# One pool of PSUM banks for attention and experts, gathers into row tiles, and a new order of the last picks

## The chip, the cores and the metric

The kernel runs on one core of one Trainium2 chip. The metric is the device time of one execution in microseconds (us), the median of several runs; smaller is better. The engines are named as in the profile: PE is TensorE, DVE is VectorE, ACT is ScalarE, POOL is GpSimd, SP is SyncE.

## The reference

The reference chains three steps over 1536 tokens of 512 features.

1. Retention-like linear attention: per head, `state = gamma * state + outer(k, v)`, `y = q @ state / 8`, over 2 batches, 8 heads, 768 positions, 64 features a head.
2. A first mixture of 8 experts with a skip: tokens with `x @ w_skip > 0` go to the expert with the largest gate logit, `relu(x @ w1) @ w2` (512 to 1024 to 512), are scaled by the gate's softmax and added to `x`; the others pass unchanged.
3. A second mixture of 8 experts on the result, without skip and without adding `x`: each expert takes its tokens in their order up to a capacity of 384, and the rest become zero.

```python
logits = xc @ w_gate
e_idx = np.argmax(logits, axis=1)
...
h = np.maximum(xc[mask] @ w1[e], 0.0)
y[mask] = gate_w[mask, None] * (h @ w2[e])
...
out[do_compute] = xc + y
```

## The kernel before, in words

**Attention.** The 768 positions are six chunks of 128, each with two batches: twelve units. `attention` (L459) holds a generator `main` (L580) and calls `step_side` after each of its yields; `step_side` moves the side generators on by one step. So the order of instructions on every engine is the order in which the program text emits them, and the number of yields decides where a side step falls. The last unit emits, in this order: the matmuls with the running state (L554), a yield, the first step of chunk 5's side generator (its first logits, L256), the matmuls with v (L564), a yield.

**Routing while attention runs.** For each chunk `route_tokens` (L369) makes the side generator `sink` (L370). Its steps are: token rows and gate logits of each batch into the row tile `rowc` (L256, L260); `pick` (L273): maximum, mask `m` of the picked expert, softmax gate into the row tile; `mrow` (L394), the table's row numbers; `write_rows` (L320) on ACT's DMA queue, which writes the chunk's 256 rows of 580 floats to `table` in device memory; the rank of each token in its expert (`ranked`, L299), the slot `sl` and the one-hot `hot` (L354); and four matmuls (L441) that turn `hot` and `mrow` into the table's row number for each slot, added into `idacc`. `idle(n)` stands for n empty steps. After chunk 4 the first block of the first expert is gathered into `a0` (L446) with the rows known by then; the rows of chunk 5 that belong to it are added by matmuls with a one-hot `oh` (`places`, L346; `place`, L337, L341), so that the first block doesn't wait for a gather.

**Pools.** Attention's SBUF pool `a_p` and PSUM pool `psa` close with `at.close()` (L626). Then the pools for gathered blocks (`xs_p`), more raw weights (`raw2`), split weights (`w2`) and activations (`m_p`) open in the same space, and a PSUM pool `ps` for the experts. What comes first in such a pool waits until everything in the pools closed before is done, the table writes out of `rowc` among it. In both phases eight banks are used: 5 for scores, 1 for the state, 2 for the rest in attention; 3 for transposes (`t`), 3 for layer 1 (`s`), 2 for layer 2 (`o`) in the experts.

**First experts.** POOL gathers the block of each expert e from `table` by an indirect DMA (`gather`, L326, L331) into a tile of `xs_p`, in the order 1, 0, 2, 3 (L797). Per expert: layer 1 (L672) with three matmuls for each product (high and low halves of a 32-bit value, `mm3`, L663), transposes of its result and of the next expert's block (`split_T`, L649, L658), layer 2 of the expert before (L686). Weights stream through SP's queue into `raw` (L175), ACT copies the high part (L225), DVE subtracts for the low part (L233).

**Second experts.** After layer 2 of expert e, `route_b` (L698) makes the expert's result rows in `row2[e % 2]`, picks the second expert, writes the 128 rows to `table` on POOL's queue (L324) and adds the new row numbers to `idb`. The first expert of the second mixture has two blocks; the second of them consists of rows of experts 0 to 7. Rows of experts 0 to 5 come from a late gather issued by expert 6's `route_b` (L741), those of experts 6 and 7 are placed by matmuls with `ohb` (`place_b0`, L837). `load_held` (L178) lets the weight loads go on that `load_w` holds back from the 39th on. From expert 1 on, two blocks go through together (`pair_T`, `pair_layer1`, `pair_layer2`), and results leave by an indirect DMA of POOL (L307).

Of the kernel before, what the change touches and what calls it, by code (L numbers as in the profile page):

```python
# [7 lines left out]
F32 = mybir.dt.float32  # L8
# [19 lines left out]
HOLD = 38  # L28
NW, NW2 = 4, 2
AWAY = 4096.0  # L30
C_GQ, C_MASK, C_GV = 0, 512, 640
# [13 lines left out]
def kernel(  # L45
# [22 lines left out]
    a_p = at.enter_context(tc.tile_pool(name="a", bufs=2))  # L68
    psa = at.enter_context(tc.tile_pool(name="psa", bufs=2, space=bass.MemoryType.PSUM))

# [201 lines left out]

    def pick(lg, nt, ng, rm, gate_out):  # L273

# [16 lines left out]
        nc.vector.tensor_tensor(out=m, in0=t[:, :, 0:8], in1=tm.to_broadcast([128, n, 8]), op=ALU.is_equal)  # L291
        se = sm.tile([128, nt, ng, 1], F32, tag=f"se{n}", name="se")
        nc.vector.tensor_reduce(out=se, in_=ex.rearrange("p (a g) j -> p a g j", a=nt), axis=AX.X, op=ALU.add)
        se2 = sm.tile([128, nt, ng], F32, tag=f"sf{n}", name="sf")
        nc.vector.tensor_scalar(out=se2, in0=se.rearrange("p a g o -> p a (g o)"), scalar1=1e-9, scalar2=None, op0=ALU.add)
        nc.vector.reciprocal(out=gate_out, in_=se2)
        return m
# [71 lines left out]
    def route_tokens(rows, rows_p):  # L369
        def sink(c, xt, psum):  # L370
# [3 lines left out]
            def pt():  # L374
                return psum("s", 5)

# [17 lines left out]
            nc.vector.tensor_tensor(  # L394
                out=mrow, in0=m4, in1=cs[:, C_ROW + B * c:C_ROW + B * c + B].unsqueeze(2).to_broadcast([128, B, 16]), op=ALU.mult
            )
# [61 lines left out]

    def attention(a_p, ps, first, nbuf, sink, pump, g_tiles):  # L459
        units = [(c, b) for c in range(NCH) for b in range(B)]  # L460
# [4 lines left out]

        def psum(tag="m", bufs=2):
            return ps.tile([128, 512], F32, tag=tag, bufs=bufs, name=tag)

        u = ps.tile([128, 512], F32, tag="u", bufs=1, name="u")
        if pump:  # L470
            warm(psum("s", 5), 11)
        nc.tensor.matmul(out=u, lhsT=zb[:, 0:128], rhs=zb[:, 0:512], start=True, stop=True, skip_group_check=True)
# [36 lines left out]
        def scores(c, b):  # L509
            qq = ain[c][:, 0, b].rearrange("p (r t) -> p r t", r=4)  # L510
            kk = ain[c][:, 1, b].rearrange("p (r t) -> p r t", r=4)
            sa = [psum("s", 5), psum("s", 5)]
            for r in range(4):
                for j in range(2):
                    nc.tensor.matmul(  # L515
                        out=sa[j][:, 128 * r:128 * r + 128], lhsT=kk[64 * j:64 * j + 64, r, :],
                        rhs=qq[64 * j:64 * j + 64, r, :], start=True, stop=True,
                    )
                if r == 1:
                    yield  # L520
            p = []
            for j in range(2):
                t = a_p.tile([128, 4, 128], F32, tag=f"p{j}", name="p")
                nc.vector.tensor_tensor(  # L524
                    out=t, in0=sa[j].rearrange("p (r t) -> p r t", r=4),
                    in1=mask.unsqueeze(1).to_broadcast([128, 4, 128]), op=ALU.mult,
                )
                p.append(t)
            pt[c, b] = p
            yield  # L530
# [94 lines left out]
    attention(a_p, psa, first, 3, route_tokens(rowc, a_p), True, [(a_p, "g2")] + 2 * [(x_p, "xh"), (x_p, "xl")])  # L625
    at.close()  # L626

    ps = fast.enter_context(tc.tile_pool(name="ps", bufs=2, space=bass.MemoryType.PSUM))
    xs_p = fast.enter_context(tc.tile_pool(name="xs", bufs=NXS))
# [3 lines left out]

    def psum(tag="t", bufs=3):
        return ps.tile([128, 512], F32, tag=tag, bufs=bufs, name=tag)

# [35 lines left out]
    def layer1(x, kind, e, mid=None):  # L672
        h = m_p.tile([128, FF], F32, tag="h", name="h", bufs=1)
        for j in range(2):
            acc = psum("s", 3)
            w = wt[kind, e, j]
# [9 lines left out]
    def layer2(hT, kind, e, mid=None):  # L686
        acc = psum("o", 2)
        for k in range(FT):
# [9 lines left out]
    def route_b(e, xs, acc, lead, rest):  # L698
# [48 lines left out]
        yield  # L747

# [132 lines left out]
    def pair_layer1(x, e):  # L881
        hs = []
        for j in range(2):
# [3 lines left out]
            for g in (0, 2):  # L887
                acc = psum("s", 3).rearrange("p (f t) -> p f t", f=2)
                for f in range(2):
# [13 lines left out]
    def pair_layer2(hs, e):  # L903
        acc = [psum("o", 2), psum("o", 2)]
        for c in range(2):
# [7 lines left out]

    x = late[3]
    emit_out(xs2[0, 0], acc)
# [21 lines left out]
    def general(gctx):  # L937
# [15 lines left out]
        with (  # L953
            tc.tile_pool(name="ga", bufs=2) as ga_p,
            tc.tile_pool(name="gps", bufs=2, space=bass.MemoryType.PSUM) as gps,
        ):
            attention(ga_p, gps, load_chunk(0, ga_p, 2), 2, sink, False, [(ga_p, f"g2{c}") for c in range(1, NCH)])
        ps = gctx.enter_context(tc.tile_pool(name="ps2", bufs=2, space=bass.MemoryType.PSUM))
# [14 lines left out]
        def dense(w1, w2):  # L973
            for e in range(E):
# [5 lines left out]
                for g in range(NTILE // 4):  # L980
# [10 lines left out]
                    for a in range(4):  # L991
                        t = 4 * g + a
                        yp = psum("o", 2)
                        for f in range(FT):
# [128 lines left out]
```

## Time and profile before

| | us |
|---|---|
| median of 3 runs | 396.45 (396.05 to 396.46) |
| the profiled execution's own time | 396.63 |
| its span, from the first to the last instruction | 394.9 |
| PE busy in the span | 377.5 (96%) |
| DVE busy | 260.6 (66%) |
| ACT busy | 216.4 (55%) |
| POOL busy | 69.8 (18%) |

A page of the profile gives busy times, the chain of work that ended last, and groups of instructions; the trace can be asked for an engine's instructions in order of time, for waits and who released them, and for DMA issues. A line of a timeline has the start, the duration, the engine, the line of the kernel, the operation, what it writes and reads, and how many instructions it stands for; in brackets stand the idle time before it and what ended it. PEld is the loading of weights into PE, which lies beside its matmuls. Ends of matmuls are modelled: neighbours overlap by about 0.1 us.

### The profile page before, as it was taken

What the parts mean: (1) busy time and instruction counts of PE and PEld (TensorE: products, weight loads), DVE (VectorE), ACT (ScalarE), POOL (GpSimd) and SP (SyncE); (2) the same over time, 40 slices, a digit from 0 to 9 for tenths busy, and PEclk for the clock granted to TensorE, in tenths of its full rate; (3) what the DMA queues carried; (4) which work ended last, traced back from release to release, by engine and by line L of the source; (5) the groups of instructions that cost most, each with busy time, mean ns of one, the idle gap of its engine ahead of it and who ended that gap; (6) DMA issues with size and microseconds to landing.
All of it is one profiled execution on the core that took longest, in us unless ns stands there. A gap on an engine that the chain in (4) does not pass through costs nothing.

```text
span 394.9 us, 6637 instructions
## 1 busy us (share of the span) xinstructions
PE 377.5 (96%) x2616; PEld 322.9 (82%) x2616; DVE 260.6 (66%) x481; ACT 216.4 (55%) x283; POOL 69.8 (18%) x97
## 2 busy tenths in 40 slices
PE   8899999879999999999999999999999999999992
PEld 3788878667877877877778898988989899898982
DVE  2668995558999999999863868374574737455110
ACT  1547773177878777877543845545545555542201
POOL 6310010180011010000046020403013040311101
PEclk9999999999999999999999999999999999999998
DMA  8999993299999998889975486849566683320101
GB/s 301 403 420 417 377 337 147 91 343 373 374 349 337 339 365 289 338 299 314 310 274 142 176 288 233 277 146 314 175 233 187 221 285 127 139 62 0 53 2 41
DMA packets 18137, 97.69 MB, mean 247 GB/s; under 512 B 2991, under 2 KB 3119, under 8 KB 8628
## 3 DMA queue, kind: packets, MB, share of 16 engines
q1 hardware_dynamic: 12180, 80.03, 56.4%
q0 software_dynamic: 4000, 13.25, 9.8%
q10 hardware_dynamic: 1920, 3.93, 2.7%
q8 instruction: 22, 0.36, 0.3%
q14 instruction: 15, 0.12, 0.1%
HBM read 88.11 MB, written 10.14 MB: 249 GB/s over the span
## 4 chain that ended last, share of the span: by engine, by line
PE 77%; DMA 7%; issue 6%; ACT 5%; DVE 3%; POOL 1%; ACTq 0%; POOLq 0%; DVEq 0%
PE o L665 11%; PE s L665 10%; PE o L667 10%; PE s L667 10%; PE s L666 10%; PE o L666 10%; DMA cs<-in_cst_dram 4%; PE t L658 3%; PE s L256 2%; ACT hi L205 2%; DMA xs<-table,ida 2%; PE t L241 2%; PE t L876 1%; PE m L564 1%; ACT ain L502 1%
## 5 line engine op out<-in xcount | busy, mean ns | idle before, releaser
L233 DVE TENSOR_TENSOR lo<-raw,hi 128x2048 fp32r<-128x2048 f32 x60 | 136.3, 2284 | 5.9 <-ACT hi L225 4.5
L225 ACT ACTIVATE hi<-raw 128x2048 fp32r<-128x2048 f32 x60 | 114.8, 1914 | 18.1 <-PE o L667 15.3
L665 PE MATMUL o<-hi,hTh 128*128 128x512 f32 x192 | 78.2, 407 | 0.2 <-ACT hTh L361 0.2
L667 PE MATMUL o<-hi,hTl 128*128 128x512 f32 x192 | 75.5, 393 | 0.0
L666 PE MATMUL o<-lo,hTh 128*128 128x512 f32 x192 | 74.9, 390 | 0.0
L666 PE MATMUL s<-xl,hi 128*128 128x256 f32 x224 | 63.2, 282 | 0.0
L667 PE MATMUL s<-xh,lo 128*128 128x256 f32 x224 | 63.1, 282 | 0.0
L665 PE MATMUL s<-xh,hi 128*128 128x256 f32 x224 | 63.1, 282 | 0.0
L896 DVE SCALAR_TENSOR_TENSOR hTl<-s,hTh 128x512 fp32r<-128x512 f32 x28 | 19.4, 692 | 63.9 <-ACT hTh L895 63.9
L307 POOL DMA_INDIRECT out_dram<-y,ixo x16 | 20.4, 1275 | 143.4 <-ACT y L751 131.0
L667 PEld LDWEIGHTS o<-hi,hTl 128*128 128x128 f32 x192 | 36.0, 188 | 8.8 <-DVE hTl L362 0.7
L666 PEld LDWEIGHTS s<-xl,hi 128*128 128x128 f32 x224 | 42.7, 191 | 0.3
L665 PEld LDWEIGHTS s<-xh,hi 128*128 128x128 f32 x224 | 42.7, 191 | 0.3
L667 PEld LDWEIGHTS s<-xh,lo 128*128 128x128 f32 x224 | 42.6, 190 | 0.0
L665 PEld LDWEIGHTS o<-hi,hTh 128*128 128x128 f32 x192 | 36.1, 188 | 6.7 <-ACT hTh L361 0.5
L666 PEld LDWEIGHTS o<-lo,hTh 128*128 128x128 f32 x192 | 36.2, 188 | 6.6
L895 ACT ACTIVATE hTh<-s 128x512 fp32r<-128x512 f32 x28 | 16.7, 598 | 40.8 <-PE s L667 40.5
L665 PE MATMUL s<-hi,xh 128*128 128x512 f32 x80 | 33.4, 417 | 1.2 <-DVE xl L362 0.9
L667 PE MATMUL s<-hi,xl 128*128 128x512 f32 x80 | 31.5, 394 | 0.0
L666 PE MATMUL s<-lo,xh 128*128 128x512 f32 x80 | 31.3, 392 | 0.0
L751 ACT ACTIVATE y<-o,xs 128x512 f32<-128x512 f32 x15 | 10.3, 690 | 32.9 <-PE o L667 25.2
L524 DVE TENSOR_TENSOR p<-s,cs 128x512 f32<-128x512 f32 x24 | 15.4, 683 | 12.7 <-PE s L515 12.7
(148 smaller groups left out, 509.9 us busy)
## 6 DMA issues: line engine op xcount, KB each, us to landing
raw<-in_w1a_dram SPq DMA_DIRECT2D x16, 1024.0 KB, 6.9
raw<-in_w2a_dram SPq DMA_DIRECT2D x16, 1024.0 KB, 6.5
raw<-in_w1b_dram SPq DMA_DIRECT2D x16, 1024.0 KB, 5.6
raw<-in_w2b_dram SPq DMA_DIRECT2D x16, 1024.0 KB, 5.0
ain<-in_qkv_dram SPq DMA_DIRECT2D x10, 1024.0 KB, 10.0
table<-rowc ACTq DMA_DIRECT2D x6, 580.0 KB, 3.8
table<-row POOLq DMA_DIRECT2D x8, 290.0 KB, 6.4
ain<-in_qkv_dram SPq DMA_DIRECT2D x4, 512.0 KB, 6.0
```

Source lines behind the costliest of these rows:

```text
L205: nc.scalar.activation(out=hi[:, k], in_=r3[:, k], func=ACTF.Copy)
L225: nc.scalar.activation(out=hi, in_=r3, func=ACTF.Copy)
L233: nc.vector.tensor_tensor(out=lo, in0=r3, in1=hi.bitcast(F32), op=ALU.subtract)
L307: return nc.gpsimd.indirect_dma_start(out=dst[:, :], out_offset=bass.IndirectOffsetOnAxis(ap=idx, axis=0), in_=src, in_offset=None, bounds ...
L524: nc.vector.tensor_tensor(out=t, in0=sa[j].rearrange("p (r t) -> p r t", r=4), in1=mask.unsqueeze(1).to_broadcast([128, 4, 128]), op=ALU.mult,
L658: nc.tensor.transpose(t[:, 128 * k:128 * k + 128], src[:, w * (4 * g + k):w * (4 * g + k) + 128], ident)
L665: nc.tensor.matmul(out=acc, lhsT=a[0], rhs=w[0], start=first, stop=False)
L666: nc.tensor.matmul(out=acc, lhsT=a[0], rhs=w[1], start=False, stop=False)
L667: nc.tensor.matmul(out=acc, lhsT=a[1], rhs=w[0], start=False, stop=last)
L751: nc.scalar.activation(out=y, in_=acc, func=ACTF.Copy, scale=xs[:, GCOL + 1:GCOL + 2])
L895: nc.scalar.activation(out=hi[:, g:g + 2, :], in_=acc, func=ACTF.Relu)
L896: nc.vector.scalar_tensor_tensor(out=lo[:, g:g + 2, :], in0=acc, scalar=0.0, in1=hi[:, g:g + 2, :].bitcast(F32), op0=ALU.max, op1=ALU.subtract
```

## The change

1. One PSUM pool `ps` with four tags of 3, 2, 1 and 2 banks serves both phases; `bank` takes the tags of a use in turn. Attention's `psum` becomes `attention_bank`.
2. In the last chunk `pick` leaves the gate (sum, add, reciprocal) to a later call; gate, `mrow` and the table write of chunk 5 come behind the two `places`.
3. In chunk 4 one empty step less stands ahead of the slot numbers (L441) and of `a0`'s gather.
4. The gathers of experts 1 and 0 go into `row2[1]` and `row2[0]`, which are there from the start. Their `route_b` then works in place and leaves out the copy of the token number.
5. Expert 6's rows are no longer placed by matmuls: the late gather comes behind the update of `idb` with expert 6's rows, its range holds them, and `place_b0` has one `place` and one step less. `load_held` moves with the gather.

```diff
+BANKS = {"a": 3, "b": 2, "c": 1, "d": 2}
...
-    psa = at.enter_context(tc.tile_pool(name="psa", bufs=2, space=bass.MemoryType.PSUM))
+    ps = fast.enter_context(tc.tile_pool(name="ps", bufs=2, space=bass.MemoryType.PSUM))
+    turns = {}
+
+    def bank(name, *tags):
+
+        i = turns[name] = turns.get(name, -1) + 1
+        tag = tags[i % len(tags)]
+        return ps.tile([128, 512], F32, tag=tag, bufs=BANKS[tag], name=name)
+
+    def attention_bank(name="m"):
+        return bank(name, *{"s": "aaabb", "u": "c", "m": "d"}[name])
...
-    def pick(lg, nt, ng, rm, gate_out):
+    def pick(lg, nt, ng, rm, gate_out, later=None):
...
-        se = sm.tile([128, nt, ng, 1], F32, tag=f"se{n}", name="se")
...
-        nc.vector.reciprocal(out=gate_out, in_=se2)
+
+        def gate():
+            se = sm.tile([128, nt, ng, 1], F32, tag=f"se{n}", name="se")
...
+            nc.vector.reciprocal(out=gate_out, in_=se2)
+
+        if later is None:
+            gate()
+        else:
+            later.append(gate)
         return m
...
-            m = pick(lg, 2, 2, None, rc[:, :, GCOL:GCOL + 2])
+            later = [] if last else None
+            m = pick(lg, 2, 2, None, rc[:, :, GCOL:GCOL + 2], later)
...
-            write_rows(nc.scalar, rc, B)
-            yield
+
+            def row_numbers():
...
+                write_rows(nc.scalar, rc, B)
+
             if not last:
+                row_numbers()
+                yield
                 yield from idle(1 if c == NCH - 2 else 2)
...
                     places(oh[:, b, :], sl[:, b:b + 1], m4[:, b, 0:1])
+                later[0]()
+                row_numbers()
...
             if not last:
-                yield from idle(2 if c == NCH - 2 else 3)
+                yield from idle(1 if c == NCH - 2 else 3)
...
-    def psum(tag="t", bufs=3):
-        return ps.tile([128, 512], F32, tag=tag, bufs=bufs, name=tag)
+    def psum(name="t"):
+        return bank("e" + name, *{"t": "a", "s": "cbb", "o": "d"}[name])
...
-        nc.vector.tensor_copy(out=r2[:, IDCOL:IDCOL + 1], in_=xs[:, IDCOL:IDCOL + 1])
+        if xs is not r2:
+            nc.vector.tensor_copy(out=r2[:, IDCOL:IDCOL + 1], in_=xs[:, IDCOL:IDCOL + 1])
...
-        if e >= E - 2:
+        if e == E - 1:
             oh = sm.tile([128, 128], F32, tag="ohb", name="ohb", bufs=2)
             places(oh, sl, m[:, 0:1])
             late.append((r2, oh))
-        if e == E - 2:
-            late.insert(0, gather(numbers(idb[:, 0:1], "id0"), 1 + NT + 128 * e))
-            load_held()
         yield
...
         nc.vector.tensor_tensor(out=idb, in0=idb, in1=new[:, 0:E], op=ALU.add)
+        if e == E - 2:
+            late.append(gather(numbers(idb[:, 0:1], "id0"), 1 + NT + 128 * E - 128))
+            load_held()
         yield
...
-    xs1 = {e: gather(ida[:, e:e + 1], 1 + NT) for e in (1, 0, 2, 3)}
+    xs1 = {e: gather(ida[:, e:e + 1], 1 + NT, row2[e] if e < 2 else None) for e in (1, 0, 2, 3)}
...
-        place(acc, *late[2], False, False)
-        yield
         place(acc, late[0], ident, False, True)
...
-    x = late[3]
+    x = late[2]
```

The rest of the diff renames the calls of `psum` to the new form and gives the fallback `general` banks of its own.

## Rows read from the trace of the kernel before

**Rows 1.** Busy times by stretch: us, busy of each engine (instructions), PE clock, DMA share, GB/s.

```profile
60.00:80.00 20.00, 17.48 (x150) 14.27 (x148) 10.95 (x49) 5.45 (x13) 3.01 (x7) 1.00 0.31 109
```

**Rows 2.** PE's waits over the span: us in total, times, longest us.

```profile
PE t L658 <- DMA xs<-table,ida: 1.6, 1, 1.6
...
PE s L665 <- DVE xl L362: 0.9, 1, 0.9
```

**Rows 3.** PE's timeline between 52 and 100 us.

```profile
65.82 1.14 PE L554 MATMUL m<-ain,sbd 128*128 128x128 f32 x8
...
69.19 0.61 PE L441 MATMUL s<-mrow,hot 128*128 128x16 f32 x4
...
70.88 1.89 PE L456 MATMUL s<-zb 128*128 128x512 bf16 x8
...
73.07 0.17 PE L304 MATMUL s<-m,ones 128*128 128x16 bf16 x1
...
85.08 0.60 PE L658 MATMUL t<-cs,h 128*128 128x128 f32 x4
87.32 0.66 PE L658 MATMUL t<-cs,xs 128*128 128x128 f32 x4 [1.65 <-DMA xs<-table,ida]
```

**Rows 4.** The chain that ended last, 50 to 100 us: start, us, what.

```profile
70.64 3.83 DMA a<-table,id
...
79.34 7.94 DMA xs<-table,ida
```

**Rows 5.** DVE's timeline between 60 and 100 us.

```profile
67.28 0.61 DVE L356 TENSOR_SCALAR hot<-iota,sl 128x256 fp32r<-128x256 f32 x2
...
73.28 0.18 DVE L296 RECIPROCAL rowc<-sf 128x4 f32<-128x4 f32 x1
...
73.53 0.18 DVE L409 TENSOR_TENSOR pr<-s,m 128x32 f32<-128x32 f32 x1
...
74.55 0.29 DVE L350 TENSOR_SCALAR oh<-iota,sl 128x128 f32<-128x128 f32 x1
```

**Rows 6.** ACT's timeline between 60 and 100 us; ACTq is its DMA queue.

```profile
73.57 0.37 ACTq L324 DMA_DIRECT2D table<-rowc  x1
...
78.88 3.72 ACT L225 ACTIVATE hi<-raw 128x2048 fp32r<-128x2048 f32 x2
```

**Rows 7.** DMA issues on the page: count, KB each, median us to landing.

```profile
table<-rowc ACTq DMA_DIRECT2D x6, 580.0 KB, 3.8
table<-row POOLq DMA_DIRECT2D x8, 290.0 KB, 6.4
...
xs<-table,ida POOLq DMA_INDIRECT x15, 4.5
```

**Rows 8.** POOL's timeline between 180 and 226 us.

```profile
195.14 0.54 POOL L324 DMA_DIRECT2D table<-row  x1 [14.09 <-DVE mrowb L725]
198.30 2.37 POOL L331 DMA_INDIRECT xs<-table,id  x1 [2.62 <-PE t L745]
...
207.74 1.02 POOL L331 DMA_INDIRECT xs<-table,idbi  x1 [4.37 <-DMA table<-row]
```

**Rows 9.** DVE's timeline between 180 and 226 us.

```profile
197.39 0.15 DVE L315 CAST id<-idb 128x1 int32<-128x1 f32 x1
```

**Rows 10.** Waits of SP's DMA queue from 60 to 100 us: total, times, longest.

```profile
SPq L175 <- DMA table<-rowc: 20.1, 1, 20.1
```

**Rows 11.** SP's timeline between 60 and 100 us.

```profile
78.70 0.33 SPq L175 DMA_DIRECT2D raw<-in_w1a_dram  x1
```

**Rows 12.** PE's timeline between 186 and 226 us.

```profile
204.93 1.05 PE L341 MATMUL t<-ohb,row 128*128 128x128 f32 x8
...
207.21 1.05 PE L341 MATMUL t<-ohb,row 128*128 128x128 f32 x8
...
217.82 1.04 PE L876 MATMUL t<-cs,xs 128*128 128x128 f32 x8
```

**Rows 13.** PE's timeline between 0 and 12 us.

```profile
1.53 4.76 PE L456 MATMUL s<-zb 128*128 128x512 bf16 x11 [1.53 <-DVE zb L91]
```

More of the change, by code (lines that the diff above doesn't have):

```diff
@@ L291, in pick @@
         nc.vector.tensor_tensor(out=m, in0=t[:, :, 0:8], in1=tm.to_broadcast([128, n, 8]), op=ALU.is_equal)
-        se = sm.tile([128, nt, ng, 1], F32, tag=f"se{n}", name="se")
-        nc.vector.tensor_reduce(out=se, in_=ex.rearrange("p (a g) j -> p a g j", a=nt), axis=AX.X, op=ALU.add)
-        se2 = sm.tile([128, nt, ng], F32, tag=f"sf{n}", name="sf")
-        nc.vector.tensor_scalar(out=se2, in0=se.rearrange("p a g o -> p a (g o)"), scalar1=1e-9, scalar2=None, op0=ALU.add)
-        nc.vector.reciprocal(out=gate_out, in_=se2)
+        def gate():
+            se = sm.tile([128, nt, ng, 1], F32, tag=f"se{n}", name="se")
+            nc.vector.tensor_reduce(out=se, in_=ex.rearrange("p (a g) j -> p a g j", a=nt), axis=AX.X, op=ALU.add)
+            se2 = sm.tile([128, nt, ng], F32, tag=f"sf{n}", name="sf")
+            nc.vector.tensor_scalar(out=se2, in0=se.rearrange("p a g o -> p a (g o)"), scalar1=1e-9, scalar2=None, op0=ALU.add)
+            nc.vector.reciprocal(out=gate_out, in_=se2)
[3 more added lines that the diff above has]
+            later.append(gate)
         return m
@@ L374, in pt @@
             def pt():
-                return psum("s", 5)
+                return psum("s")
             lg = sm.tile([128, B, 17], F32, tag="lg", name="lg")
@@ L393, in sink @@
             mrow = sm.tile([128, B, 16], F32R, tag="mrow", name="mrow")
-            nc.vector.tensor_tensor(
-                out=mrow, in0=m4, in1=cs[:, C_ROW + B * c:C_ROW + B * c + B].unsqueeze(2).to_broadcast([128, B, 16]), op=ALU.mult
-            )
-            write_rows(nc.scalar, rc, B)
-            yield
+            def row_numbers():
+                nc.vector.tensor_tensor(
+                    out=mrow, in0=m4, in1=cs[:, C_ROW + B * c:C_ROW + B * c + B].unsqueeze(2).to_broadcast([128, B, 16]), op=ALU.mult
+                )
+                write_rows(nc.scalar, rc, B)
             if not last:
+                row_numbers()
+                yield
                 yield from idle(1 if c == NCH - 2 else 2)
@@ L456, in warm, with attention @@
             nc.tensor.matmul(out=acc, lhsT=zb[:, 0:128], rhs=zb[:, 0:512], start=True, stop=True)
-    def attention(a_p, ps, first, nbuf, sink, pump, g_tiles):
+    def attention(a_p, psum, first, nbuf, sink, pump, g_tiles):
         units = [(c, b) for c in range(NCH) for b in range(B)]
@@ L511, in scores @@
             kk = ain[c][:, 1, b].rearrange("p (r t) -> p r t", r=4)
-            sa = [psum("s", 5), psum("s", 5)]
+            sa = [psum("s"), psum("s")]
             for r in range(4):
@@ L624 @@
             nc.gpsimd.memset(t[:, :, KW * k + 128:KW * k + KW], 0.0)
-    attention(a_p, psa, first, 3, route_tokens(rowc, a_p), True, [(a_p, "g2")] + 2 * [(x_p, "xh"), (x_p, "xl")])
+    attention(a_p, attention_bank, first, 3, route_tokens(rowc, a_p), True, [(a_p, "g2")] + 2 * [(x_p, "xh"), (x_p, "xl")])
     at.close()
-    ps = fast.enter_context(tc.tile_pool(name="ps", bufs=2, space=bass.MemoryType.PSUM))
     xs_p = fast.enter_context(tc.tile_pool(name="xs", bufs=NXS))
@@ L674, in layer1 @@
         for j in range(2):
-            acc = psum("s", 3)
+            acc = psum("s")
             w = wt[kind, e, j]
@@ L686, in layer2 @@
     def layer2(hT, kind, e, mid=None):
-        acc = psum("o", 2)
+        acc = psum("o")
         for k in range(FT):
@@ L887, in pair_layer1 @@
             for g in (0, 2):
-                acc = psum("s", 3).rearrange("p (f t) -> p f t", f=2)
+                acc = psum("s").rearrange("p (f t) -> p f t", f=2)
                 for f in range(2):
@@ L903, in pair_layer2 @@
     def pair_layer2(hs, e):
-        acc = [psum("o", 2), psum("o", 2)]
+        acc = [psum("o"), psum("o")]
         for c in range(2):
@@ L956, in general, with general_bank @@
         ):
-            attention(ga_p, gps, load_chunk(0, ga_p, 2), 2, sink, False, [(ga_p, f"g2{c}") for c in range(1, NCH)])
+            def general_bank(name="m"):
+                return gps.tile([128, 512], F32, tag=name, bufs={"s": 5, "u": 1, "m": 2}[name], name=name)
+            attention(ga_p, general_bank, load_chunk(0, ga_p, 2), 2, sink, False, [(ga_p, f"g2{c}") for c in range(1, NCH)])
         ps = gctx.enter_context(tc.tile_pool(name="ps2", bufs=2, space=bass.MemoryType.PSUM))
@@ L992, in dense @@
                         t = 4 * g + a
-                        yp = psum("o", 2)
+                        yp = psum("o")
                         for f in range(FT):
```

6 lines of the change are left out of this document (2 added, 4 removed).

## Prediction

> **What bounds the kernel now.** I read the busy times by stretch first. TensorE (PE) is busy for 17.5 us in the stretch from 60 to 80 us, where attention ends and the experts begin [rows 1]; the waits that the trace names for it elsewhere are all under a microsecond or lie in the first chunks. So a microsecond taken from PE's path counts in full, and what another engine saves counts only where PE waits for it. The list of PE's waits says where that is [rows 2]: its longest is 1.6 us for the first gathered block of tokens. On PE's timeline the transposes of that block (line 658) begin at 87.32, though the work ahead of them in PE's queue had ended by 85.08 + 0.60 = 85.7 [rows 3]. The chain of waits gives the same place: the block of 128 rows that POOL asks for at 79.34 lands 7.94 us later, while the gather of `a0`, with the DMA engines to itself, took 3.83 [rows 4]. So two questions decide: when is that gather issued, and what else is moving then?
>
> **Chunk 4's slot numbers (`idle(1)` in place of `idle(2)`).** The four small matmuls of line 441 move one step forward in PE's queue: behind the 554 group, which ends at 65.82 + 1.14 = 66.96, and ahead of chunk 5's first logits and of the value matmuls [rows 3]. They need `hot`, which VectorE (DVE) ends at 67.28 + 0.61 = 67.89 [rows 5]. The first half of `hot` is there at about 67.65, so PE stands for 0.7 us, and the group (0.6, stretched to 0.8 by the second half) ends at 68.45. Everything queued behind it on PE, and all that ACT and DVE derive from it, is then 1.4 us later. Nothing gives this back: before, the same group filled PE's wait for `xt` (69.19 to 69.80). In return `a0` can be gathered sooner, but that gather also waits for chunk 4's table write, so it gains a few tenths at most. PE's stand before `a0`'s matmuls disappears, since PE itself now arrives later.
>
> **The last pick (`later`).** The rank matmuls of chunk 5 end at 73.07 + 0.17 = 73.24, but `pr` starts at 73.53, behind the gate's reciprocal and `mrow` [rows 3, 5]. Without these in front it starts about 0.27 sooner, which with the 1.4 makes 74.66. From `pr` to the second `oh` it is 1.02 (73.53 to 74.55), and the reciprocal now comes three small operations of 0.2 later: 74.66 + 1.02 + 0.6 = 76.3, against 73.28. So the table write of chunk 5, issued by ACT at 73.57 right behind the reciprocal [rows 6], goes out at 76.6. A table write lands 3.8 us after its issue [rows 7]: 80.4, against 77.4. The placed block itself is 0.2 us later; it feeds expert 0, whose end PE only used to wait for the gather, so this 0.2 costs nothing while the wait lasts.
>
> **First blocks into `row2`.** A gather into `row2` no longer waits for the attention pools to be given back, only for its indices (ready before 79) and for the table, which it reads. Before, the table was there at 77.4 and the pools decided; afterwards the table decides, at 80.4. From the last release to the issue POOL takes some 0.76 where the release is of this kind (index cast ends at 197.39 + 0.15, gather at 198.30) [rows 8, 9], so the gather goes out at 81.15 instead of 79.34. Its flight is the unknown: 3.83 alone, 7.94 beside weights [rows 4]. Which? SP's next two weight loads wait for the same table write [rows 10] and then for the last placing matmul, and went out at 78.70, 0.64 ahead of the gather [rows 11]. Released by the write at 80.4, they are again some 0.6 ahead. I take 7.94: landing at 89.1, PE's transposes there instead of 87.32, **+1.75**. The lower end: with a flight of 3.83 the block lands at 85, but ACT's conversions, which began at 78.88 in a pool that opens with the same release [rows 6], also start at 80.5; three of 1.9 and three splits of 0.5 stand in front of the block's split, which then begins at 87.7 instead of 88.0. So this term lies between **-0.35** and +1.75. The copies of the token number that fall away (0.15 of DVE each) lie beside PE's work: nothing.
>
> **Weights.** The two loads go out 1.9 us later, and the stream behind them shifts by about as much as PE does. The waiting loads' data are consumed one or two experts later, so I count nothing; if that cover were gone, the price would be the 0.2 by which the stream slips more than PE.
>
> **One pool of banks.** The numbers of banks per use stay the same (3, 3, 2). The experts' first matmul waited 0.9 us for `xl`, not for a bank [rows 2]. Nothing; if a bank of attention were still held there, it would be at most the time of one reader, 0.4.
>
> **Expert 6's rows gathered.** One `place` less: the groups of line 341 take 1.05 each and overlap their neighbours by 0.1 [rows 12], and this stretch is PE's path: **-0.95**. The two one-hot operations less on DVE (0.4) are beside PE. The price: the late gather now needs expert 6's table write. That was issued at 195.14 [rows 8] and a row write takes 6.4 to land [rows 7]: 201.5, so the gather goes out at 202.3 instead of 198.30. The gathers of its kind fly 4.5 in the median [rows 7]; with a weight load moving, 4.5 to 5.5: 206.8 to 207.8. PE wants it at the step that is free now, 207.21 [rows 12]. I take a stand of **+0.3**; the ends are 0 and, at 7.94, 3.0. On POOL's queue, expert 7's table write and the gathers of the second blocks stand behind the late gather and move by up to 3 us (the first that needs the write went out at 207.74 [rows 8]); its block is transposed at 217.82 [rows 12], so a flight of 4.5 still hides. The held weight loads move in the text of SP's queue only, past nothing of SP's own.
>
> **Sum.** +1.75 - 0.95 + 0.3 = +1.1 us. The profiled execution took 396.63, of which 394.9 are its span, 0.2 above the median of 396.45. Counted from the median: **397.5 us**; its own range is 397.0 to 398.2.
>
> **Rivals.**
>
> *The gather escapes the weights (faster).* Place: the DMA engines between 81 and 87 us. Its flight falls towards 3.83, PE is bound by ACT's split, and the `place` is saved: -0.35 - 0.95 = -1.3, so 395.2. For it: the two issues are only 0.6 us apart. Against it: they were as far apart before, and the flight was 7.94. It decides when the flight is under 6 us: then the block lands before 87.2, and the sum is under -0.8.
>
> *The terms cancel.* The flight is 6.3 to 7.2, since the first rows meet less traffic, and the late gather lands in time: +0.1 to +1.0 for the first term, about 0 in the sum: 396.5.
>
> *The clock falls.* PE stands from 85.9 to 89.1, 3.2 us, twice as long as before. The eleven opening matmuls show a cold start: 4.76 us [rows 13], where eight of the same shape took 1.89 at 70.88 [rows 3], so about 0.2 more for each of ten. If expert 1's layer begins like that, it costs 2.0: +3.1 in all, 399.6. Before, the stand of 1.6 us was followed by matmuls at full pace, so this would be new. The Trainium skill (TensorE: Matmul & The Clock Gate, "HAM oscillation — how this bites in real kernels") says that a long enough wait for a transfer sends the array back to half rate, and that each such wait pays for the return; by it the sum would be this rival's 399.6. No row here shows a fall between matmuls.
>
> *The late gather is late.* A flight of 7.94 there too: PE stands 3.0 at the placed block, +3.8, 400.2. Against it: one load is moving then, not two.
>
> **Chances.** Forecast 0.40; terms cancel 0.25; clock 0.15; gather escapes 0.12; late gather 0.08. A measurement of this kernel can tell 0.2%, 0.8 us, from no change. Slower by more: nearly all of the forecast, the clock and the late gather, 0.58; within: the cancelling case and the forecast's low edge, 0.28; faster: the escape and what is cheaper still, 0.14. The range leaves out the late gather and half of the escape: 395.4 to 399.6.
>
> **What would show it.** Line 441's chunk-4 group at about 67.7 with a wait for `hot`; chunk 5's table write at 76.6; the gather into `row2` at about 81.1, released by the table and not by PE; the transposes of that block near 89; two groups of line 341 in the late placing, the gather's without a long wait. The forecast is wrong if the gather goes out before 80, if its flight is under 6 us, or if PE's gaps before 90 us do not grow.

## The result, and the profile after

| | median us (lowest to highest, runs) | ratio to before |
|---|---|---|
| before, same chip | 396.27 (396.05 to 396.58, 6) | |
| after | 399.60 (399.05 to 402.19, 6) | 1.0094, 95% interval 1.0066 to 1.0123 |

The change costs 3.3 us where the forecast had 1.1; the median lies on the upper edge of the range. Three words are used all the way: PE's *stand* is the idle time of PE in front of the first gathered block, a gather's *flight* the time from its issue to its landing (seen here as the start of what waited for it), and the *granted clock* the share of full speed that PE is given, in a stretch or, as the mean, in a whole run. The profiled execution is the longest of the six (402.19, span 400.4): 1.5 to 2 us of its times below are its own, most of it a late landing of constants in the first chunk (PE's 2.3 us for `idw`), so single steps are better read from the experiments.

The list of PE's waits after (us in total, times, longest), to be set against [rows 2]:

```profile
PE et L679 <- DMA row<-table,ida: 3.8, 1, 3.8
PE s L267 <- POOL idw L136: 2.3, 1, 2.3
...
PE s L267 <- DVE p L546: 0.9, 1, 0.9
...
PE s L267 <- DVE idacc L469: 0.5, 1, 0.5
```

PE's timeline after, around the change (L466 is the L441 of before, L359 its L341, L679 its L658, L686 to L688 its L665 to L667):

```profile
68.33 1.14 PE L576 MATMUL m<-ain,sbd 128*128 128x128 f32 x8
70.20 0.76 PE L466 MATMUL s<-mrow,hot 128*128 128x16 f32 x4 [0.73 <-DVE hot L374]
...
77.03 1.14 PE L359 MATMUL m<-cs,a 128*128 128x128 f32 x8
...
92.11 1.11 PE L679 MATMUL et<-cs,row 128*128 128x128 f32 x4 [3.78 <-DMA row<-table,ida]
...
94.50 0.63 PE L687 MATMUL es<-lo,xh 128*128 128x512 f32 x1
```

POOL's and SP's timelines there, the first gather and the first weight load behind it:

```profile
84.02 1.06 POOL L349 DMA_INDIRECT row<-table,ida  x1 [6.21 <-DMA table<-rowc]
```
```profile
83.52 0.33 SPq L186 DMA_DIRECT2D raw<-in_w1a_dram  x1
```

Busy times and granted clock (PEclk) by stretch, after:

```profile
core 0: us, PE busy (x) PEld busy (x) DVE busy (x) ACT busy (x) POOL busy (x), PEclk, DMA share, GB/s
84.00:88.00 4.00, 2.98 (x15) 2.21 (x14) 2.60 (x2) 4.00 (x4) 3.37 (x3) 1.00 0.88 311
88.00:92.00 4.00, 0.32 (x3) 0.08 (x1) 2.60 (x2) 2.37 (x3) 3.39 (x3) 0.87 1.01 388
92.00:96.00 4.00, 3.89 (x13) 3.23 (x14) 2.11 (x2) 2.74 (x3) 1.07 (x2) 0.50 1.02 394
96.00:100.00 4.00, 4.00 (x15) 3.16 (x15) 3.58 (x3) 1.31 (x3) 0.00 (x0) 0.77 0.97 346
100.00:104.00 4.00, 4.00 (x21) 3.34 (x20) 1.36 (x2) 3.71 (x4) 0.00 (x0) 1.00 0.99 410
```

Three things are to be seen. First, the wait for `hot` (0.73), the gather released by the table and the loads ahead of it are there as forecast. Second, PE stands 3.8 us, and behind that its clock is at half, 1.2 GHz, in all of 92 to 96, and matmuls of 0.39, as expert 0's are here, take 0.63. Third, attention has two waits that PE's list of before doesn't have, for `p` and for `idacc`: nothing in the forecast touches them. Late in the kernel, PE's timeline shows two groups at L359 instead of three and no wait at the second:

```profile
211.78 1.05 PE L359 MATMUL et<-ohb,row 128*128 128x128 f32 x8
214.05 1.05 PE L359 MATMUL et<-cs,xs 128*128 128x128 f32 x8
```

### The profile page after: what moved, and what is told of

Same layout as the page of the kernel before. It is cut to its first block, busy times and chain, and to the rows that moved or that the text cites. A ratio compares the mean times of both kernels' runs of the same rounds, so it can differ in the third digit from the quotient of the medians.

```text
span 400.4 us, 6620 instructions
## 1 busy us (share of the span) xinstructions
PE 379.1 (95%) x2608; PEld 323.8 (81%) x2608; DVE 260.3 (65%) x477; ACT 216.3 (54%) x283; POOL 68.6 (17%) x97
## 4 chain that ended last, share of the span: by engine, by line
PE 73%; DVE 8%; DMA 7%; issue 7%; ACT 3%; POOL 0%; POOLq 0%; ACTq 0%; DVEq 0%
PE es L686 10%; PE es L687 10%; PE es L688 10%; PE eo L686 10%; PE eo L688 10%; PE eo L687 10%; DMA cs<-in_cst_dram 4%; PE et L679 3%; PE s L267 2%; DMA row<-table,ida 2%; PE et L252 2%; DVE lo L228 1%; PE et L896 1%; PE s L537 1%; ACT hi L216 1%
## 5 line engine op out<-in xcount | busy, mean ns | idle before, releaser
L686 PE MATMUL eo<-hi,hTh 128*128 128x512 f32 x192 | 77.9, 406 | 0.3 <-ACT hTh L379 0.3
L688 PE MATMUL eo<-hi,hTl 128*128 128x512 f32 x192 | 75.6, 394 | 0.1
L687 PE MATMUL eo<-lo,hTh 128*128 128x512 f32 x192 | 75.0, 390 | 0.0
L687 PE MATMUL es<-xl,hi 128*128 128x256 f32 x224 | 63.1, 281 | 0.0
L688 PE MATMUL es<-xh,lo 128*128 128x256 f32 x224 | 63.0, 281 | 0.0
L686 PE MATMUL es<-xh,hi 128*128 128x256 f32 x224 | 63.0, 281 | 0.0
L688 PEld LDWEIGHTS eo<-hi,hTl 128*128 128x128 f32 x192 | 36.0, 188 | 8.6 <-DVE hTl L380 0.7
L687 PEld LDWEIGHTS es<-xl,hi 128*128 128x128 f32 x224 | 42.6, 190 | 0.3
L686 PEld LDWEIGHTS es<-xh,hi 128*128 128x128 f32 x224 | 42.6, 190 | 0.3
L688 PEld LDWEIGHTS es<-xh,lo 128*128 128x128 f32 x224 | 42.6, 190 | 0.0
L686 PEld LDWEIGHTS eo<-hi,hTh 128*128 128x128 f32 x192 | 36.1, 188 | 6.9 <-ACT hTh L379 0.5
L687 PEld LDWEIGHTS eo<-lo,hTh 128*128 128x128 f32 x192 | 36.2, 188 | 6.8
L686 PE MATMUL es<-hi,xh 128*128 128x512 f32 x80 | 34.2, 427 | 0.0
L688 PE MATMUL es<-hi,xl 128*128 128x512 f32 x80 | 32.0, 401 | 0.0
```

What stands on the lines that cost most here:

```text
L686: nc.tensor.matmul(out=acc, lhsT=a[0], rhs=w[0], start=first, stop=False)
L687: nc.tensor.matmul(out=acc, lhsT=a[0], rhs=w[1], start=False, stop=False)
L688: nc.tensor.matmul(out=acc, lhsT=a[1], rhs=w[0], start=False, stop=last)
```

## The experiments

Sixteen kernels, each beside runs of the kernel before on the same chip (medians of before: 396.31, 396.42, 396.31 and 396.57 in the four sets e1 to e4, e5 to e8, e9 to e12, e13 to e16). Theory at the start: the pool of banks was not free, and a fallen clock added the rest. Rival: the orders alone cost more than the sum had.

### The clock, and the two orders (on the kernel after)

**e1_fill**: PE works on zeros while it waits (`warm` emits that many matmuls on a tile of zeros).

```diff
         if e == 0:
             next(turn)
+            warm(psum(), 14)
```

> The changed kernel with 14 idle-work matmuls (zeros, 128x512, into a free bank) between the transposes of expert 0's first result and those of expert 1's block, where PE stood 3.8 us in the changed kernel's trace and its granted clock then fell to 0.50. Theory 1 (of the 3.3 us lost, about 2.0 are the clock): the granted clock stays at 1.00 between 84 and 104, expert 1's first layer takes 5.9 us as before instead of 7.4, and the time is about 2 us under the changed kernel's 399.6: 397.4 to 398.0. Theory 2 (the clock only coincides; the late gather alone costs 3.3): the time stays at 399 to 400, since PE still waits for the same landing. In both the gather still goes out 0.7 after the table write of chunk 5 has landed.

Measured: 398.19 (397.93 to 398.44), ratio 1.0045, 1.0032 to 1.0059. PE's timeline and the stretches:

```profile
86.08 3.19 PE L481 MATMUL et<-zb 128*128 128x512 bf16 x14
89.75 0.66 PE L679 MATMUL et<-cs,row 128*128 128x128 f32 x4 [0.48 <-DMA row<-table,ida]
```
```profile
88.00:92.00 4.00, 3.27 (x17) 1.73 (x16) 1.62 (x3) 1.85 (x3) 2.69 (x3) 1.00 1.00 369
92.00:96.00 4.00, 4.00 (x18) 3.31 (x19) 4.00 (x3) 2.87 (x4) 0.00 (x0) 1.00 1.03 392
```

The clock stays full and 1.4 of the 3.3 us are gone, though PE still waits for the block behind the zeros (0.48). The expectation had 2.0 for the clock; the remaining 1.9 are not the clock.

**e2_idle_back, e3_gate_back, e4_orders_back**: chunk 4's empty step back; the gate and the table write back in front of the `places`; both.

```diff
-                yield from idle(1 if c == NCH - 2 else 3)
+                yield from idle(2 if c == NCH - 2 else 3)
...
-            m = pick(lg, 2, 2, None, rc[:, :, GCOL:GCOL + 2], later)
+            m = pick(lg, 2, 2, None, rc[:, :, GCOL:GCOL + 2])
...
+            row_numbers()
...
-                later[0]()
-                row_numbers()
```

> The changed kernel with chunk 4's second empty step put back. Theory (1.4 us of the delayed table write come from PE's wait for hot): chunk 5's logits, pick, table write and the gather into the row tile come 1.4 us earlier, PE stands about 2.2 instead of 3.8, the clock stays up, so that 1.4 of the wait and the 2.0 of the clock come back: 396.0 to 396.8. If the order of the slot numbers costs nothing, the time stays at 399 to 400. If the clock falls all the same, 398.

> The changed kernel with the last pick in its old order: gate, row numbers and the table write of chunk 5 ahead of the ranks. Theory: the table write goes out 1.6 us earlier relative to the pick, the gather with it, PE stands about 2.1, the clock stays up: 395.8 to 396.8. If the write's place is not what releases the gather, the time stays at 399 to 400. The placed first block comes some 0.3 us later, which is not seen in the time.

> Both orders put back: what is left of the change are the one pool of banks, the row tiles and the gathered rows of expert 6. Theory: the table write is again 3.8 us under way before the indices are ready, so the gather waits for the indices alone and goes out about 0.5 us ahead of the kernel before's; expert 0's layer starts about 1 us earlier because of the banks, which the gather's landing hides; one place less saves 0.95. Sum 1.2 to 1.6 under the kernel before: 394.7 to 395.1. Rival (the parts left over cost something of their own): at or above the kernel before, 396.3 or more.

Measured: 397.90 (ratio 1.0035, 1.0021 to 1.0049), 397.66 (1.0036, 1.0017 to 1.0055) and 396.82 (1.0009, 0.9994 to 1.0024). Each order alone gives back 1.7 to 1.9, both 2.8: less than the two added, since with either left PE still stands (3.3 and 3.1 us) and the clock still falls (0.51 and 0.57 in 88 to 92). All three lie above the times first expected of them: the clock fell with either order back, and with both back the kernel should have been faster than before by a placing group and more, but isn't (the rival of e4). Something else in it costs, and in all four kernels the 554 group of chunk 5, at 65.82 in [rows 3], begins at 66.8 or later.

### The pool of banks (on the kernel before)

**e5_banks_only**: part 1 of the change alone, its diff as above.

> The kernel before with one edit: the one pool of PSUM banks. Theory 1 (the bank pool costs about 1.0 us inside attention, by other waits on a bank's last reader, and lets expert 0's layer start earlier, so PE's stand before the first gathered block grows): the 554 group that began at 65.82 begins at 66.7 to 66.9, the gathered block's transposes begin at 87.9 to 88.6 instead of 87.32, and the whole takes 397.0 to 397.8. Theory 2 (the pool costs nothing, as the prediction had it, and the drift in attention comes from the row tiles or from expert 6's gather): that group stays at 65.8 and the time at 396.1 to 396.6.

Measured: 398.89 (397.64 to 400.15, 9 runs), ratio 1.0060, 1.0041 to 1.0079: **2.5 us for the part costed at nothing.** The places are those of theory 1, the time is 1.1 above its upper end. PE's timeline (L267 is the L256 of before, L562 its L554, L665 its L658, L673 its L666):

```profile
38.02 1.25 PE L267 MATMUL s<-idw,xt 128*128 128x145 f32 x8 [0.50 <-DVE idacc L455]
...
52.51 0.76 PE L267 MATMUL s<-idw,xt 128*128 128x145 f32 x4 [0.90 <-DVE p L532]
...
63.16 1.61 PE L267 MATMUL s<-idw,xt 128*128 128x145 f32 x8
...
66.81 1.14 PE L562 MATMUL m<-ain,sbd 128*128 128x128 f32 x8
...
79.33 0.48 PE L672 MATMUL es<-hi,xh 128*128 128x512 f32 x1
...
88.21 0.66 PE L665 MATMUL et<-cs,xs 128*128 128x128 f32 x4 [2.68 <-DMA xs<-table,ida]
...
89.89 0.60 PE L673 MATMUL es<-lo,xh 128*128 128x512 f32 x1
```

Before has other waits in the place of the first two, and its first matmul of expert 0 waits:

```profile
PE s L256 <- ACT rowc L260: 1.0, 2, 0.7
```
```profile
79.49 0.50 PE L665 MATMUL s<-hi,xh 128*128 128x512 f32 x1 [0.94 <-DVE xl L362]
```

Two mechanisms stand in it. In attention PE is about 1.0 later by 66.81: 0.2 up to 50 us, 0.65 up to 62 us, behind the wait for `p`, and the rest inside the group at 63.16, which takes 1.61 where the same group of before takes 1.25. The bank numbers in the built programs say why: before, scores, row sums and ranks share one ring of five, and the tile of the second wait gets the bank of an earlier row sum, which ACT has read (`rowc`); with the turn `aaabb` over rings of three and two it gets the bank of the scores of the same step, which DVE reads later (`p`). So does the second tile of the group at 63.16. The tile of the first wait gets the bank of a rank tile, whose last reader is `idacc`. The banks of a ring are not taken in a fixed round, so rings of three and two in turn are not a ring of five: the number of banks is the same, but not who held the bank last. The second mechanism: expert 0's first matmul no longer waits, it begins right behind the last `place`, and PE, done sooner, stands 2.7 us instead of the 1.65 of [rows 3]. The clock falls (matmuls at 0.60 and 0.63; 0.74 in 88 to 92).

**e10_five_ring**: the same with one ring of five.

```diff
-BANKS = {"a": 3, "b": 2, "c": 1, "d": 2}
+BANKS = {"a": 5, "c": 1, "d": 2}
...
-        return bank(name, *{"s": "aaabb", "u": "c", "m": "d"}[name])
+        return bank(name, *{"s": "a", "u": "c", "m": "d"}[name])
...
-        return bank("e" + name, *{"t": "a", "s": "cbb", "o": "d"}[name])
+        return bank("e" + name, *{"t": "a", "s": "caa", "o": "d"}[name])
```

> One pool of banks on the kernel before, as in e5_banks_only, but the five banks of the scores and row sums are one ring instead of a ring of three and a ring of two taken in turn; the experts take from that ring too. PE's waits in attention are then those of the kernel before, and only the experts' start differs. Theory 1 (the split ring costs attention its 1.0 us, and the earlier start of expert 0's layer only lengthens PE's stand, which brings the clock down): the 554 group at 65.8, expert 0's first matmul at 78.2 to 78.6, PE's stand 2.4 to 2.9, first matmuls of expert 1 at 0.63, 397.3 to 397.9. Theory 2 (a stand of 2.6 does no harm): the same places, granted clock 0.99 or more, 396.2 to 396.7. Rival (the split is not the cause of the drift in attention): the 554 group at 66.7 or later, 397.6 to 399.

Measured: 396.29 (395.35 to 397.75, 12 runs), ratio 0.9986, 0.9965 to 1.0007. PE's timeline:

```profile
65.76 1.14 PE L562 MATMUL m<-ain,sbd 128*128 128x128 f32 x8
...
78.23 0.47 PE L672 MATMUL es<-hi,xh 128*128 128x512 f32 x1
...
87.38 0.66 PE L665 MATMUL et<-cs,xs 128*128 128x128 f32 x4 [2.96 <-DMA xs<-table,ida]
...
89.06 0.40 PE L673 MATMUL es<-lo,xh 128*128 128x512 f32 x1
...
218.71 0.60 PE L665 MATMUL et<-cs,h 128*128 128x128 f32 x4
```

The split of the ring was the cause in attention: with one ring the 1.0 is gone, and every tile of attention has the bank that it has before. Expert 0's layer starts 1.26 before the 79.49 of before and gains nothing, since the block lands where it did. The last line is new: the same group of before waited for a reader of its bank; here its bank is free, and it starts 0.74 sooner.

```profile
219.45 0.66 PE L658 MATMUL t<-cs,h 128*128 128x128 f32 x4 [0.59 <-DVE hTl L362]
```

The clock held in this execution behind a stand of 2.96. The twelve runs fall apart by their mean granted clock: at 0.995 they take 395.35 to 395.94, at 0.991 and 0.992 396.26 to 397.01, at 0.988 and 0.990 397.7. So both theories came true, each in some executions.

**e14_banks_fill**: e5 with `warm(psum(), 11)` in the place of e1's line.

> e5_banks_only (398.89) with 11 matmuls on the zero tile in the same place. Theory 1 (the pool of banks costs two things, 0.9 to 1.0 in attention and 1.3 to 1.6 by the clock after the longer stand): clock 1.00 in every stretch from 84 to 104, 397.1 to 397.5. Rival (the pool costs a third thing behind the first experts): clock full and 397.8 to 398.8.

Measured: 397.74 (397.51 to 399.08), ratio 1.0022, 1.0006 to 1.0038; clock 1.00 in every stretch from 84 to 104, and the block's transposes at 88.32. The pool is 1.2 above before with a full clock, 2.5 without: about 1.0 is attention, 1.2 to 1.3 the clock, and 0.2 stays open. The median is 0.2 above the expectation, on a chip where before took 396.57; no third cost shows in the waits.

### The forecast's own terms (on the kernel before)

**e9_no_banks**: the kernel after without part 1, that is parts 2 to 5 of the change.

> The changed kernel without the one pool of banks: row tiles, both orders and expert 6's gather alone. Theory 1 (the prediction's terms for the orders and the placing were right, and PE's stand of about 3 us brings the clock down here too): the first block's transposes at 88.7 to 89.3, granted clock under 0.9 in 88 to 96, 398.2 to 398.9. Theory 2 (the terms were right, and the clock falls only with the bank pool): the same place for the transposes, clock 0.99 or more, 397.0 to 397.5. Rival (the orders cost only together with the bank pool): 395.0 to 396.0.

Measured: 398.28 (397.45 to 400.00), ratio 1.0035, 1.0015 to 1.0055. PE's, POOL's and ACT's timelines (L455 is the L441 of before, L672 its L658, L679 to L681 its L665 to L667):

```profile
67.69 0.76 PE L455 MATMUL s<-mrow,hot 128*128 128x16 f32 x4 [0.73 <-DVE hot L363]
...
89.02 1.12 PE L672 MATMUL t<-cs,row 128*128 128x128 f32 x4 [3.31 <-DMA row<-table,ida]
...
91.41 0.63 PE L680 MATMUL s<-lo,xh 128*128 128x512 f32 x1
...
92.18 0.40 PE L679 MATMUL s<-hi,xh 128*128 128x512 f32 x1
```
```profile
80.86 1.06 POOL L338 DMA_INDIRECT row<-table,ida  x1 [5.68 <-DMA table<-rowc]
```
```profile
76.54 0.37 ACTq L331 DMA_DIRECT2D table<-rowc  x1
```

These are the forecast's steps almost to the tenth: 67.7, a write at 76.6, a gather at 81.15, the block at 89.1. What the sum did not hold is the clock, at half until 92 (0.58 in 88 to 92). The time is as theory 1 had it.

**e13_no_banks_fill**: e9 with `warm(psum(), 13)` in the place of e1's line.

> e9_no_banks (398.28) with 13 matmuls on the zero tile behind the first transposes of expert 0's hidden block, so that PE works while it waits for the gathered block. Theory 1 (the 1.1 us by which e9_no_banks is over the prediction's sum is the clock): transposes of the block still at 88.8 to 89.2, granted clock 1.00 in every stretch from 84 to 104, 397.0 to 397.5, the prediction's own sum without the pool of banks. Rival (the late gather costs further on too, beyond PE's stand): the clock is full and the time 397.8 to 398.4.

Measured: 397.74 (397.24 to 399.54), ratio 1.0022, 1.0004 to 1.0040; clock 1.00 from 84 to 108. Four of the twelve runs lie where theory 1 had them, the median is 0.24 above it. In the profiled execution (398.3) the block landed 1.2 later than in e9, at 90.23, though the gather went out at 80.99: the flight varies from one execution to the next, by about a microsecond between these two. So the clock is worth 0.5 to 0.8 here; the rest above 397.2 may be a spread of the flight, which no run here takes apart. Against its own before the kernel with a held clock and without the pool is 1.2 slower, near the forecast's whole sum of 1.1, though the 0.3 for a late gather in that sum did not come (e6, next).

**e6_place_only, e7_rows_only, e11_rows_place**: part 5 alone, part 4 alone, both; their diffs as above.

> The kernel before with one edit: expert 6's rows are gathered, with one placing group less. Theory 1 (this part alone is worth the placing group, as the prediction's term had it): 395.3 to 395.6, the late gathered block placed without a wait, nothing different ahead of 190 us. Rival (the late gather, which now needs expert 6's table write, lands late): PE stands 0.3 to 3.0 at its placing, 395.8 to 398.4.

> The kernel before with one edit: the first two gathers go into the row tiles. Theory 1 (the order of the last picks made the gather late, not the row tiles): POOL issues the gather at 78.4 to 78.8, released by the index cast, ahead of or beside the loads; with a flight of 7.9 the block lands 0.6 to 0.9 earlier than the 87.28 of before, so 395.4 to 395.8. Rival (what is saved in the wait for the attention pools is lost in the flight, as the loads still take the DMA engines at 78.7): the block at 87.1 to 87.4, 396.1 to 396.5.

> The kernel before with two parts of the change, the row tiles and expert 6's gather. Theory (the two gains are at two places and add up): 394.4 to 394.9, block's transposes at 86.3 to 86.6, one placing group less, clock 0.99 or more. Rival (what is won at 86 us is given back before 200, since the weights' stream is where it was): 395.2 to 395.6.

Measured: 395.52 (395.19 to 398.40), ratio 0.9988, 0.9966 to 1.0010; 395.55 (395.15 to 395.85), 0.9970, 0.9957 to 0.9983; 394.74 (394.38 to 397.80), 0.9961, 0.9933 to 0.9989. By the medians each gains 0.9, and together 1.6. The interval of e6 alone takes in no change (three of its twelve runs have the lower clock); its trace shows the gain, POOL's gather and PE's placing of it:

```profile
201.60 1.06 POOL L331 DMA_INDIRECT xs<-table,id  x1 [6.24 <-DMA table<-row]
```
```profile
206.90 1.05 PE L341 MATMUL t<-cs,xs 128*128 128x128 f32 x8
```

No wait: the gather has landed 5.3 us after its start at the latest. In e7 POOL's and PE's timelines:

```profile
78.38 1.03 POOL L331 DMA_INDIRECT row<-table,ida  x1 [4.64 <-DVE ida L315]
```
```profile
86.44 0.66 PE L658 MATMUL t<-cs,row 128*128 128x128 f32 x4 [1.05 <-DMA row<-table,ida]
```

The gather no longer waits for attention's pools, goes out 0.96 before the 79.34 of [rows 4] and lands 0.88 sooner. So the row tiles help; only the late table write made the gather into them late.

### The flight of 8 us

**e8_loads_after, e12_one_load_after**: the raw2 weight loads wait for the first block, both of them (on e4_orders_back), or only the second (on e11_rows_place).

```diff
+    scratch = dram.tile([1, RW], F32, name="scratch")
...
+    nc.sync.dma_start(out=scratch[0:1, :], in_=row2[1][0:1, :])
     for _ in range(NRAW2):
         load_w()
```

> Both orders back as in e4_orders_back (396.82), and one more edit: a read of one line of the first gathered block stands ahead of the first raw2 weight loads in SP's queue, so that these loads start when the block has landed. Theory 1 (the flight of 7.9 is the two loads beside it): flight 3.8 to 4.6, block landed at 83.6 to 84.4, PE's stand before its transposes at most 0.6, no granted clock under 0.95 from 84 to 100, first layer of expert 1 about 1.5 earlier; whole time 395.0 to 395.9. Rival A (the loads, 5 us later, now arrive late for an expert further on): the early gain is there but 396.5 to 398. Rival B (the flight does not depend on them): block at 87.6 as before, time as e4 or slower.

> As e11_rows_place, and the second of the two raw2 loads waits until the first gathered block has landed (a read of one line of it stands ahead of that load in SP's queue). Theory 1 (one load beside the gather takes half the traffic away: flight 5.5 to 6.5, block at 84.2 to 85.2, PE's stand 0 to 0.4, and a slip of 5 us in one load is covered): 393.6 to 394.3. Rival (the load's data are wanted at about 100, as e8_loads_after's stand there showed): the block's gain is there, and 395 to 397 all the same. Rival (the flight stays at 7.9): 394.4 to 396.

Measured: 399.22 (398.04 to 402.38), ratio 1.0096, 1.0058 to 1.0133, and 396.78 (394.80 to 399.03), 1.0003, 0.9983 to 1.0022. In e8 SP's, PE's and ACT's timelines:

```profile
83.18 0.24 SPq L818 DMA_DIRECT2D scratch<-row  x1
```
```profile
85.34 0.60 PE L677 MATMUL et<-cs,row 128*128 128x128 f32 x4
...
107.75 1.06 PE L253 MATMUL et<-idw,x2t 128*128 128x8 f32 x8 [1.81 <-ACT x2t L737]
```
```profile
102.52 1.91 ACT L237 ACTIVATE hi<-raw 128x2048 fp32r<-128x2048 f32 x1 [1.68 <-DMA raw<-in_w1a_dram]
...
107.10 0.60 ACT L737 ACTIVATE x2t<-et 128x512 f32<-128x512 f32 x1
```

Issued at 79.69, the block is there when the read behind it goes out at 83.18: a flight of at most 3.5, and no stand before its transposes. In e12, with one load beside it, the gather is issued at 78.62 and the read goes out at 84.43: at most 5.8, as its theory 1 had it, and no stand either. The loads make the 8. But they then come late: ACT's conversions wait for them (1.68), and `x2t` queues behind them, so PE waits at 107.75: its idle time is moved by 20 us. One load late does the same, for 2.2 us, and in that profile the clock falls there (0.83 in 104 to 108):

```profile
84.43 0.24 SPq L801 DMA_DIRECT2D scratch<-row  x1
```
```profile
106.56 1.83 PE L242 MATMUL t<-idw,x2t 128*128 128x8 f32 x8 [2.23 <-ACT x2t L719]
```

So the rival of late loads came true in both; e8's median lies above its range too, four of its six runs having a mean clock of 0.991 or less.

### What beats both kernels

**e16_five_rows_place, e15_five_rows_place_fill**: e10's ring, row tiles, expert 6's gather; the second with `warm(psum(), 8)` in e1's place.

> One ring of five banks, row tiles and expert 6's gather, with 8 matmuls on the zero tile in PE's stand. Theory (gains add: 0.7 to 0.8 at 219 us from the ring, 0.9 each from the row tiles and the placing group, and the clock holds): 393.7 to 394.3. Rival (the ring's gain at 219 us goes, as the waits there fall otherwise when a placing group is gone): 394.5 to 394.9.

> The same without the 8 matmuls. Theory (PE stands about 2.1 us, and as in e4_orders_back and e10_five_ring the clock then falls in a part of the executions): lowest runs as e15's, the median 0.5 to 1.5 above it, with mean granted clocks of 0.991 to 0.993 in the slower ones. Rival (the stand is short enough): no difference to e15_five_rows_place_fill.

Measured: e16 393.96 (393.37 to 395.43, 9 runs), ratio 0.9928, 0.9907 to 0.9950; e15 **393.80 (393.74 to 394.10, 6 runs), ratio 0.9920, 0.9895 to 0.9945**, 2.8 us under before by the medians. PE's timeline of e15:

```profile
84.11 1.89 PE L467 MATMUL et<-zb 128*128 128x512 bf16 x8
86.48 0.66 PE L665 MATMUL et<-cs,row 128*128 128x128 f32 x4 [0.49 <-DMA row<-table,ida]
...
217.07 0.60 PE L665 MATMUL et<-cs,h 128*128 128x128 f32 x4
```

The gains add, and the matmuls on zeros buy steadiness: without them five runs of e16 (mean clock 0.997) take 393.37 to 393.96, four (0.990 to 0.993) 394.84 to 395.43. The profiled execution of e16 is one of the four, with 0.57 in 88 to 92 behind a stand of 2.4. The medians are only 0.2 apart, where 0.5 to 1.5 was expected, and the five are shorter than e15's runs: the filling costs 0.2 to 0.4 where the clock would have held.

## Why the forecast was wrong in size

The direction and the place were right, and the mechanism that the sum was built on came as described. Against [rows 3 to 7], in e9:

- *Chunk 4's slot numbers, the last pick, the gather into a row tile*: forecast +1.75 at the block's transposes; measured 89.02 against 87.32, **+1.70**. The choice of the long flight was right: 8.2, with the loads ahead, and e8 and e12 show that they are what makes it long. (That PE's other waits behind the first chunks are all under a microsecond was misread: before's list has 1.3 for `a`, at 74.52. Chunk 4's order uses that wait up, so that expert 0's layer begins in e9 where it did in before, at 79.51.)
- *Expert 6's rows*: forecast -0.95 and +0.3 for a late gather. The second term did not come: e6 gains 0.9 and PE doesn't wait. The gather went out at 201.60 instead of 202.3 (0.3 of it is e6's earlier schedule), and had landed by 206.90.
- *Weights*: nothing, as forecast; when the loads are later by more than the 1.9 of the forecast, as in e8, that cover is gone.
- **The step that failed: "One pool of banks ... Nothing (at most 0.4)".** It counted banks per use and looked for a bank still held at the change of phase. Alone, this part costs 2.5 (e5): about 1.0 inside attention, through who held each bank last (e5 against e10), and 1.2 to 1.3 by the clock (e5 against e14). The same step read the experts' 0.9 us wait for `xl` as a wait for data. It was one for banks: the second half's `xl` reads a bank of `psa`, and `ps` could open only behind it. With one pool that wait is gone (e5, e10), which sounds like a gain and, with the block landing where it did, only lengthens PE's stand.
- *The clock*: a rival at 0.15, with 2.0 us. It came, at a price of **1.4** (e1). The argument against it, that matmuls ran at full pace behind the stand of 1.6, rested on one profiled execution: 25 of 107 runs of before beside these experiments have a mean granted clock of 0.991 or 0.992, and take some 1.5 us longer than the others. The price of 2.0 took ten matmuls at 0.2 each; after and in e5 seven or eight run at 0.60 or more. That this rival's 399.6 is the measured time is luck: its price was 0.6 too high, the forecast's 0.3 for a late gather did not come, and the 1.0 in attention made up for both.

The sum with the measured terms: 1.7 (orders and row tiles) - 0.9 (place) + 1.0 (banks in attention) + 1.4 (clock) = 3.2, against the measured 3.3. The pool alone (2.5, e5) and the rest alone (2.0, e9) add up to more than 3.3: the clock falls in both, and together it is paid for once.

The clock term can be read across the kernels (but for e8 and e12, whose long wait is elsewhere). PE's stand is the one in the profile, the share that of runs with a mean granted clock of 0.994 or more:

| kernel | stand, us | runs at 0.994 or more |
|---|---|---|
| e11, e7 | 0.8, 1.05 | 7 of 8, 12 of 12 |
| e6, before | 1.5, 1.65 | 9 of 12, 82 of 107 |
| e4, e16, e5, e10 | 2.1, 2.4, 2.7, 2.96 | 3 of 11, 5 of 9, 1 of 9, 5 of 12 |
| e3, e2, e9, after | 3.1, 3.3, 3.3, 3.8 | 1 of 12, 1 of 6, 0 of 12, 0 of 6 |
| e1, e13, e14, e15 (filled) | 0.5, 1.6, 0.3, 0.5 | 5 of 5, 11 of 12, 12 of 12, 6 of 6 |

That the loss lies behind this stand is shown in the profiled executions of after, e2 to e5, e9 and e16, and by the fills; of a run without a profile only the mean is known. The Trainium skill (TensorE: Matmul & The Clock Gate, "HAM oscillation — how this bites in real kernels") has it that a long wait for a transfer sends the array back to half rate, each time it comes. The rows at 0.63 agree; e10's profiled execution, with 0.40 behind 2.96 us, shows that behind such a stand it need not come every time.

## What to carry to other kernels

When PSUM pools are merged or a ring is split, list for each tile of the critical engine who read its bank last, before and after: the count of banks says nothing about it, and a ring of five is not a ring of three and one of two. An engine made earlier in front of a wait that stays is not a gain: its stand grows, and on PE a longer stand can cost the clock behind it (1.2 to 1.4 us in e5 and after); with matmuls on zeros in the stand, 34 of 35 runs kept a mean clock of 0.994 or more, for 0.2 to 0.4 us where it would have held anyway. Before costing a rival low because one profile doesn't show it, look at the granted clocks of the other runs.

## What was not expected of the hardware

PE's clock behind stands of 2 to 3 us is not the same in every execution of one kernel: five of e10's twelve runs have a mean clock of 0.995, and the three groups of its runs differ by about 1 us each. The first gather's flight is at most 3.5 us with the loads behind it (e8), at most 5.8 with one load of 1 MB beside it (e12), 7.8 to 8.2 with two in the profiles of the other kernels, and 9.2 in that of e13.
